# Top-k attention into a Fourier mixer: first scores from half of the queries and keys on two queues, and the tails' products padded to the full array

## The chip, the cores and the metric

The kernel runs on one core of a Trainium2 chip. The metric is device time in microseconds (us), as the median of several executions. The profile comes from one further execution. The engines of the core are TensorE (PE, with its weight loads listed as PEld), VectorE (DVE), ScalarE (ACT), GpSimd (POOL) and SyncE (SP), which issues most DMA transfers.

## The reference

All tensors are 32-bit floats. There are 8 batches, 8 heads, 576 tokens and a head size of 64. In the attention block each row of scores keeps its 32 largest entries:

```python
scores = scale * np.matmul(q, k.transpose(0, 1, 3, 2))          # 576 x 576 for each of 64 heads
kth = np.partition(scores, -32, axis=-1)[..., -32:-31]
scores = np.where(scores >= kth, scores, -1e9)
attn = np.exp(scores - scores.max(-1, keepdims=True))
attn = attn / (attn.sum(-1, keepdims=True) + 1e-9)
x = np.matmul(attn, v)                                           # -> (8, 576, 512)
```

The second block takes the real part of a two-dimensional Fourier transform over tokens and channels, adds it, normalises, and applies a two-layer MLP of 512 x 2048:

```python
u = x + np.real(np.fft.fft(np.fft.fft(x, axis=1), axis=2))
un = (u - u.mean(-1, keepdims=True)) / np.sqrt(u.var(-1, keepdims=True) + 1e-6)
out = u + np.maximum(un @ w_ch1, 0.0) @ w_ch2
```

## The kernel before, in words

**Tiles.** Two heads form a pair; there are 32 pairs, four to a batch. The 576 tokens of a head are two halves of 288, and each half is cut into two full blocks of 128 and a tail of 32. So a pair has full blocks 0 to 3 for each head, and block 4, which holds the tails. The tails' queries of both heads are handled as one item of 64 rows. A pair therefore has nine items (`IN_PAIR`), and the kernel walks over 288 items, one to a step of its main loop.

**One item.** `scores` (L274) multiplies queries by keys. Part 0 gives the scores against the four full key blocks (L329, and L314 for the tails' item from the second batch on). Part 1 (L299) gives the scores against the tails' keys of both heads at once: the right operand is `kt_t`, a block-diagonal 128 x 128 tile. For the tails' item its left operand has 64 columns, for others 128. ACT copies the scores from PSUM into the tile S (L332, L303). Then `top_ops` finds the 32 largest of each row on DVE, by four MAX8 (L350) and three MATCH_REPLACE8 (L352). `bounds` (L359, POOL) makes the thresholds `nt`; `mask` uses ACT (L366) and POOL (L367); `expo` is ACT's exponent (L373). `transposes` (L394, L405, L409) turns the result on PE, and `attend` (L431) multiplies by v.

**Order.** The schedule is written out by hand. In each step the program emits, engine by engine, the work of several items: the scores of item i+3, the first two top-k rounds of item i+1 and the last two of item i, the mask, the exponent, and work planned with `at(step, where, fn, cost)`. The loop fills PE up to a planned time per step (`level`) with pieces of the previous batch's MLP (`hidden`, L737, and `back`, L761 and L797). Each engine runs its own instructions in program order. In steps 0 to 33 the weights are also loaded and converted from 64-bit words: ACT writes `wh` (L169) and two more parts (L185, L188), DVE shifts (L176), POOL joins (L195, L196).

**Queries and keys.** `load_nat` brings the q or k of a pair into `nat_t`, one buffer that both share, with four transfers of 64 KB (`load_full`, L213) and four of 8 KB for the tails (`load_tails`, L224). `prep` (L239) transposes it on PE (L248) and copies it to `qT` (L256) or to `kT` (L258) and `kt_t` (L261) on ACT. Pair 0's k has a buffer of its own, `kn0`. At the start SP issues q of pair 0, the tails of pair 0's k, three weight pieces, v, then q of pair 1, and then the constants `fs`, `fd`, `sg` and two more weight pieces. ACT issues the identity and the full blocks of pair 0's k after its function table load (L844). In the loop, the q of the next pair is prepared in the first step of a pair.

**Token transform.** `dft_tokens` (L579) is called twice for a batch (even and odd frequencies). It multiplies folded tokens by the table `fs`: twelve products of 128 output rows and three with a single one. The third block of each sum is the tails', which has 64 rows; `fold_tails` (L535) writes it. ACT copies the result to `y` (L627 to L629), which `dft_channels` (L639) uses on PE (L651).

In the profile each of these matmuls appears as two passes, each with its own weight load.

Of the kernel before, what the change touches and what calls it, by code (L numbers as in the profile page):

```python
# [9 lines left out]
F32 = mybir.dt.float32  # L10
# [8 lines left out]
P = 128  # L19
TH = 32  # L20
# [44 lines left out]
def kernel(  # L65
# [9 lines left out]
    nc = tc.nc  # L75
    B, H, S, D = q.shape
# [4 lines left out]
    NC = 5  # L81
# [41 lines left out]
    nat_t = const.tile([P, NC, 2, D], F32, name="nat", tag="nat")  # L123

    kt_t = const.tile([P, P], F32, name="kt", tag="kt")
    v_t = [const.tile([P, NC, 2, D], F32, name=f"v{i}", tag=f"v{i}") for i in range(2)]


# [76 lines left out]

    def load_full(dst, src, pair, queue=None):
        b, hp = divmod(pair, NPB)
        for e in range(2):  # L210
            s2 = src[b, 2 * hp + e].rearrange("(h r) d -> h r d", h=2)
            for h in range(2):
                (queue or nc.sync).dma_start(  # L213
                    out=dst[:, 2 * h:2 * h + 2, e, :],
                    in_=s2[h, 0:2 * P, :].rearrange("(t p) d -> p t d", p=P),
                )

    def load_tails(dst, src, pair, row0=(0, 0)):
        b, hp = divmod(pair, NPB)
        for e in range(2):  # L220
            s2 = src[b, 2 * hp + e].rearrange("(h r) d -> h r d", h=2)
            for h in range(2):
                r0 = row0[e] + TH * h
                nc.sync.dma_start(out=dst[r0:r0 + TH, NF, e, :], in_=s2[h, 2 * P:HS, :])  # L224

    def load_nat(n, pair, dst=None, queue=None):
        if pair < NPAIR:
            nat[n, pair] = nat_t if dst is None else dst
            src = q if n == "q" else k
            load_full(nat[n, pair], src, pair, queue)  # L230
            load_tails(nat[n, pair], src, pair)

    def load_v(pair):
# [2 lines left out]
            load_full(v_of[pair], v, pair)  # L236
            load_tails(v_of[pair], v, pair, (0, TAIL))

    def prep(n, pair):  # L239

        if pair >= NPAIR:
            return 0.0
        src = nat.pop((n, pair))
        t_sb = attp.tile([P, S if n == "q" else NF * P], F32, name=f"{n}T_{pair}", tag=f"{n}T")
        for c0, c1 in ((0, NF), (NF, NC)):
            tp = ps_t.tile([P, 4, P], F32, name=f"tp{n}_{pair}_{c0}", tag="tp")
            for c in range(c0, c1):
                nc.tensor.transpose(  # L248
                    tp[:, c - c0, :], src[:, c, :, :].rearrange("p h d -> p (h d)"), ident
                )  # L250
            if c0 == 0:
                dst, got = t_sb[:, 0:NF * P], tp.rearrange("p a c -> p (a c)")
            else:
                dst, got = t_sb[:, NF * P:], tp[:, 0, 0:TAIL]
            if n == "q":
                nc.scalar.mul(out=dst, in_=got, mul=scale)  # L256
            elif c0 == 0:
                nc.scalar.copy(out=dst, in_=got)  # L258
            else:
                for hd in (slice(0, D), slice(D, P)):  # L260
                    nc.scalar.copy(out=kt_t[hd, hd], in_=got[hd])  # L261
        (qT_of if n == "q" else kT_of)[pair] = t_sb
        return 0.7


# [8 lines left out]
    def scores(i, part):  # L274

        if not 0 <= i < N:
            return 0.0
        pair, t, e = items[i]  # L280
        qT, kT = qT_of[pair], kT_of[pair]
        rows = ROWS[t]
        if part == 0:
            for n in range(1 if e is None else 2):
                Ssb[i + n] = attp.tile([P, S], F32, name=f"S_{i + n}", tag="S", bufs=6)
        q_cols = slice(P * t, P * t + rows)


        plain = (slice(0, NF * P), slice(NF * P, S))
        if e is None:  # L290
            to = [(Ssb[i], slice(TAIL * h, TAIL * (h + 1)), *plain) for h in range(2)]
        else:
            to = [
                (Ssb[i], slice(0, P), *plain),
                (Ssb[i + 1], slice(0, P), slice(TAIL, S), slice(0, TAIL)),
            ]
        if part == 1:
            sp = ps_s.tile([P, NF * P], F32, name=f"sp_{i}_t", tag="sp")
            nc.tensor.matmul(  # L299
                sp[0:rows, 0:P], lhsT=qT[:, q_cols], rhs=kt_t, start=True, stop=True  # L300
            )
            for h, (s_t, r, _, tails) in enumerate(to):
                nc.scalar.copy(out=s_t[r, tails], in_=sp[0:rows, TAIL * h:TAIL * (h + 1)])  # L303
            return 0.3
        if e is None and i >= PER_BATCH:

            half = NF * P // 2
            sps = [
                ps_s.tile([P, NF * P], F32, name=f"sp_{i}_{h}", tag="sp") for h in range(2)
            ]  # L310
            for g in range(2):
                for h in range(2):
                    hd = slice(D * h, D * (h + 1))
# [12 lines left out]
        for h, (s_t, r, keys, _) in enumerate(to):  # L326
            hd = slice(D * h, D * (h + 1))
            sp = ps_s.tile([P, NF * P], F32, name=f"sp_{i}_{h}", tag="sp")
            nc.tensor.matmul(  # L329
                sp[r], lhsT=qT[hd, q_cols], rhs=kT[hd, :], start=True, stop=True  # L330
            )
            nc.scalar.copy(out=s_t[r, keys], in_=sp[r])  # L332
        return 1.04
# [174 lines left out]
        return ap.rearrange("p (m two) -> p two m", two=2)  # L508

    Q1, Q2, Q3 = DM // 4, DM // 2, 3 * DM // 4  # L510
    ROWS3 = (P, P, TAIL)
    folded, ft_of, y_of, yt_of, us_of, rs_of, unT_of = ({} for _ in range(7))

    def fold_channels(eng, z, f, n):

# [18 lines left out]

    def fold_tails(b, eng):  # L535


        z = batp.tile([P, DM], F32, name=f"zt_{b}", tag="fold_s")[0:TAIL]
        ft_of[b] = batp.tile([P, DM + 1], F32, name=f"ft_{b}", tag="fold_t")
        f = ft_of[b][0:TAIL]  # L540
        fold_halves(eng, x_of[b][0:TAIL, 4, :], z)
        for n in range(2):
            fold_channels(eng, z, f[:, 0:DM], n)
        eng.tensor_copy(out=f[:, DM:DM + 1], in_=z[:, Q1:Q1 + 1])
# [34 lines left out]
    def dft_tokens(b, par):  # L579
# [1 line left out]
        while any(u[2] == "hidden" for u in queue):  # L581
            one_unit()
        _, zw, fg = folded[b, par]
        tails = ft_of[b]
        if b not in y_of:
            y_of[b] = batp.tile([P, 4, S], F32, name=f"y_{b}", tag="y")
        y = y_of[b]
# [4 lines left out]
        def mm(g2, gg, st, lhsT, rows, table, start=False):  # L592

            nc.tensor.matmul(  # L594
                yps[g2][0:rows, gg, :],
                lhsT=lhsT[0:ROWS3[st]],
                rhs=fs[0:ROWS3[st], table, par, st, :],
                start=start,
                stop=st == 2,
                skip_group_check=True,  # L600
            )

        for g2 in range(2):
            for gg in range(2):
                g = 2 * g2 + gg
                for st in range(2):
                    mm(
                        g2, gg, st, fg[:, st, P * g:P * (g + 1)], P, gg,  # L610
                        start=gg == 0 and st == 0,
                    )
        for st in range(2):
            mm(0, 1, st, zw[:, st, Q1:Q1 + 1], 1, 0)
        mm(0, 1, 2, tails[:, DM:DM + 1], 1, 0)
        for g2 in range(2):
            for gg in range(2):
                g = 2 * g2 + gg
                mm(g2, gg, 2, tails[:, P * g:P * (g + 1)], P, gg)

        mir, back = (
            (slice(HS + 2, S, 2), slice(KQ - 2, 0, -1)) if par == 0
# [218 lines left out]
    nc.vector.memset(cc[:, 0:1], -1.0)  # L841

    warm = small.tile([P, 1], F32, name="warm", tag="rd", bufs=6)
    nc.scalar.activation(out=warm, in_=cc[:, 0:1], func=AF.Exp)  # L844
    nc.vector.memset(cc[:, 1:2], FAR)
    for t in mv + den_t:
        nc.vector.memset(t, 1.0)

    kn0 = batp.tile([P, NC, 2, D], F32, name="kn0", tag="y")
    for t in v_t:  # L850
        nc.gpsimd.memset(t[TAIL:P, NF, 0, :], 0.0)
        nc.gpsimd.memset(t[0:TAIL, NF, 1, :], 0.0)
    for t in (nat_t, kn0):
        nc.gpsimd.memset(t[TAIL:P, NF, :, :], 0.0)
    nc.gpsimd.memset(kt_t, 0.0)

    nc.scalar.dma_start(out=ident, in_=id_d.ap())
    load_nat("q", 0)
    load_nat("k", 0, kn0, nc.scalar)
    prep("q", 0)  # L860
    prep("k", 0)


# [14 lines left out]
    for n in range(3):  # L878
        load(n)
    load_v(0)  # L880
    load_nat("q", 1)
    nc.sync.dma_start(out=fs, in_=fs_d.ap())
    nc.sync.dma_start(out=fd, in_=fd_d.ap())
    nc.sync.dma_start(out=sg, in_=sg_d.ap())
# [139 lines left out]
            got += one_unit()  # L1024
        return got

    for j in (0, 2):
        for c in range(2):
            scores(j, c)
    for op in top_ops(0, (0, 1)):  # L1030
        op()
    i, carry = 0, 0.0
# [144 lines left out]
```

## Time and profile before

| | |
|---|---|
| median of 8 executions | 1956.56 us (1955.75 to 1957.84) |
| profiled execution | 1956.7 us |
| its span, from first to last instruction | 1954.9 us |
| granted TensorE clock, mean | 0.972 |
| first MAX8 on DVE | 12.45 us after the span's start |
| first pass of the first token transform | 241.92 us |

The span is what the profiler's rows cover; the execution's own time is 1.8 us longer. A row of the timeline gives start, length, engine, line, operation, output and inputs; for PE the first shape, such as 128\*64, is the part of the array that is used (rows \* columns). What stands in brackets is the engine's idle time before the row and what ended it. `PEld` rows are weight loads, rows with a q after the engine (`SPq`) are its queue's instructions. Passes overlap in time, so the start of the next pass, not the end of the last one, tells what a pass costs.

### The profile page before, as it was taken

The numbers are of one execution on the slowest core, as the hardware profiler recorded it, in microseconds if no ns is written. First come the engines' busy times: TensorE is split into PE (matmuls) and PEld (weight loads), VectorE is DVE, ScalarE is ACT, GpSimd is POOL, SyncE is SP. The second block draws the span as 40 slices with busy tenths as digits, with TensorE's granted clock in tenths as the row PEclk, the third lists the DMA queues.
The fourth block names the chain that finished last, engine by engine and source line by source line (L and its number), as shares of the span: only waits on it lengthen the run. The fifth ranks groups of instructions, "written<-read, shape, count | busy, mean of one in ns | idle before, by whom it ended". The sixth has DMA issues, their size and how long they took to land.

```text
span 1954.9 us, 27234 instructions
## 1 busy us (share of the span) xinstructions
PE 1842.3 (94%) x8626; PEld 1116.0 (57%) x8626; DVE 1576.8 (81%) x3240; ACT 1202.6 (62%) x3063; POOL 773.3 (40%) x1056
## 2 busy tenths in 40 slices
PE   6566699999999999999999999999999999998999
PEld 3334465464655656556564756556564756566655
DVE  7999989998999989888888879988888879843000
ACT  6878657776766667666666657666666657541100
POOL 4768642326523444235523444235522444232000
PEclk8787799999999999999999999999999999999999
DMA  5333000101001010010100110010000100000000
GB/s 156 107 94 105 19 13 19 33 19 29 19 19 33 19 26 16 13 33 19 29 19 19 27 24 18 13 33 19 24 18 25 27 24 19 1 14 1 11 14 11
DMA packets 133583, 57.80 MB, mean 30 GB/s; under 512 B 124352, under 2 KB 124480, under 8 KB 133440
## 3 DMA queue, kind: packets, MB, share of 16 engines
q1 hardware_dynamic: 132208, 55.73, 10.6%
q8 instruction: 69, 1.13, 0.2%
q14 instruction: 74, 0.61, 0.1%
q10 hardware_dynamic: 1232, 0.33, 0.1%
HBM read 46.57 MB, written 9.44 MB: 29 GB/s over the span
## 4 chain that ended last, share of the span: by engine, by line
PE 80%; POOL 7%; DVE 6%; issue 3%; ACT 3%; DMA 0%; SPq 0%; POOLq 0%; DVEq 0%; ACTq 0%
PE hp L737 24%; PE cp L761 22%; PE o L431 7%; PE tpP L394 6%; PE sp L329 6%; PE yp L594 3%; PE cp L797 3%; POOL wk L367 2%; PE mp L651 2%; DVE m L350 2%; DVE wk L352 2%; PE sp_t L299 2%; POOL w L196 2%; POOL w L195 2%; PE tpk L248 1%
## 5 line engine op out<-in xcount | busy, mean ns | idle before, releaser
L367 POOL TENSOR_TENSOR wk<-S,wk 128x576 f32<-128x576 f32 x288 | 407.0, 1413 | 919.2 <-ACT wk L366 865.6
L350 DVE MAX8 m<-wk 128x8 f32<-128x576 f32 x864 | 623.4, 749 | 5.5
L737 PE MATMUL hp<-unT,w 128*128 128x256 f32 (+1 forms) x2048 | 539.5, 410 | 2.5 <-ACT unT L718 2.1
L761 PE MATMUL cp<-w,hT 128*128 128x512 f32 x1024 | 478.4, 599 | 0.0
L737 PEld LDWEIGHTS hp<-unT,w 128*128 128x128 f32 x2048 | 373.4, 191 | 126.6 <-issue 32.3
L352 DVE MATCH_REPLACE8 wk<-m,wk 128x576 f32<-128x576 f32 x576 | 427.6, 742 | 0.0
L761 PEld LDWEIGHTS cp<-w,hT 128*128 128x128 f32 x1024 | 179.3, 190 | 182.3 <-issue 181.5
L373 ACT ACTIVATE wk<-wk,nt 128x576 f32<-128x576 f32 x288 | 224.8, 781 | 53.6 <-POOL wk L367 52.2
L394 PE MATMUL tpP<-ident,wk 128*128 128x128 f32 x1152 | 185.3, 285 | 67.3 <-ACT wk L373 45.1
L397 ACT COPY PT<-tpP 128x512 f32<-128x512 f32 (+1 forms) x320 | 171.0, 545 | 123.8 <-PE tpP L394 121.3
L366 ACT ACTIVATE wk<-S,nt 128x576 f32<-128x576 f32 x288 | 226.9, 788 | 27.0 <-POOL nt L359 25.8
L394 PEld LDWEIGHTS tpP<-ident,wk 128*128 128x128 f32 x1152 | 139.7, 145 | 166.9 <-ACT wk L373 63.4
L350 DVE MAX8 m<-S 128x8 f32<-128x576 f32 x288 | 214.0, 743 | 22.6 <-ACT S L303 22.3
L741 ACT ACTIVATE hT<-hp 128x320 f32<-128x320 f32 (+1 forms) x256 | 104.7, 409 | 197.4 <-PE hp L737 195.1
L352 DVE MATCH_REPLACE8 wk<-m,S 128x576 f32<-128x576 f32 x288 | 213.7, 742 | 0.0
L431 PE MATMUL o<-PT,v 128*64 128x256 f32 (+3 forms) x1440 | 193.4, 411 | 2.2 <-ACT PT L397 1.7
L332 ACT COPY S<-sp 128x512 f32<-128x512 f32 (+1 forms) x264 | 141.9, 588 | 65.9 <-PE sp L329 65.7
L329 PE MATMUL sp<-kT,qT 64*128 64x512 f32 (+1 forms) x528 | 161.0, 671 | 3.6 <-ACT means L916 3.1
L431 PEld LDWEIGHTS o<-PT,v 128*64 128x64 f32 x1440 | 110.1, 151 | 75.0 <-issue 16.1
L775 DVE SCALAR_TENSOR_TENSOR x<-cp,gi,x 128x512 f32<-128x512 f32 x11 | 8.2, 746 | 128.3 <-PE cp L761 128.3
L299 PEld LDWEIGHTS sp_t<-kt,qT 128*128 128x128 f32 (+1 forms) x322 | 51.3, 186 | 58.4 <-issue 22.2
L329 PEld LDWEIGHTS sp<-kT,qT 64*128 64x128 f32 (+1 forms) x528 | 42.7, 192 | 60.8 <-issue 44.7
(124 smaller groups left out, 1797.5 us busy)
## 6 DMA issues: line engine op xcount, KB each, us to landing
space<-in_moe_w_ch_dram SPq DMA_DIRECT2D x32, 512.0 KB, 3.6
nat<-in_q_dram SPq DMA_DIRECT2D x128, 64.0 KB, 2.1
v<-in_v_dram SPq DMA_DIRECT2D x128, 64.0 KB, 2.1
out_dram<-x SPq DMA_DIRECT2D x32, 256.0 KB, 2.1
nat<-in_k_dram SPq DMA_DIRECT2D x124, 64.0 KB, 2.1
nat<-in_q_dram SPq DMA_DIRECT2D x128, 8.0 KB, 1.7
v<-in_v_dram SPq DMA_DIRECT2D x128, 8.0 KB, 1.7
nat<-in_k_dram SPq DMA_DIRECT2D x124, 8.0 KB, 1.7
```

What stands on the lines that cost most here:

```text
L329: nc.tensor.matmul(sp[r], lhsT=qT[hd, q_cols], rhs=kT[hd, :], start=True, stop=True)
L332: nc.scalar.copy(out=s_t[r, keys], in_=sp[r])
L350: ops.append(lambda src=src, m8=m8: nc.vector.max(out=m8, in_=src))
L352: ops.append(lambda src=src, m8=m8: nc.vector.match_replace(w, m8, src, NEG))
L366: nc.scalar.activation(out=w, in_=Ssb[i], func=AF.Relu, scale=-FAR, bias=Nt[i][:, 1:2])
L367: nc.gpsimd.tensor_tensor(out=w, in0=Ssb.pop(i), in1=w, op=ALU.subtract)
L373: nc.scalar.activation(out=w, in_=w, func=AF.Exp, bias=Nt.pop(i)[:, 0:1], accum_out=den_t[pair % 3][:, c:c + 1],)
L394: nc.tensor.transpose(tp[:, c, :], p_sb[:, k0 + P * c:k0 + P * (c + 1)], ident)
L397: nc.scalar.copy(out=pt[:, NF * he:NF * (he + 1), col:col + w], in_=tp[:, :, o:o + w])
L431: nc.tensor.matmul(o[D * e:D * (e + 1), c0:c1], lhsT=vv[:, c, e, :], rhs=pt[:, 2 * NF if c == NF else NF * e + c, c0:c1], start=(c == 0), ...
L737: nc.tensor.matmul(hp[:, 0:w], lhsT=w1[:, dt, P * it:P * (it + 1)], rhs=unT[:, dt, 0:w], start=(dt == 0), stop=(dt == NDT - 1),)
L761: nc.tensor.matmul(cp, lhsT=hT[:, it, P * n:P * (n + 1)], rhs=w2[:, it, :], start=(it == 0), stop=(it == NIT - 1),)
```

## The change

The start is put in another order. Of pair 0, SP now issues the first halves of q, the first halves of k, one head's k tails, the second halves of q and the q tails; ACT issues the identity, the second halves of k and the other head's k tails, and all this before ACT's function table is loaded. `prep` is split, so that only query blocks 0 and 1 are transposed ahead of the first scores; blocks 2, 3 and the tails follow after the scores of items 0 and 1. The q loads of pair 1 are emitted after that, and so stand on SP behind `fs`, `fd`, `sg` and the two weight pieces. Item 0's product with the tails' keys uses another PSUM pool and is copied by DVE. The memsets of `nat_t`, `kn0` and `kt_t` go from POOL to DVE.

The tails' item takes the last 128 columns of `qT` as its left operand, so that its 64 rows come out as rows 64 to 127. The tails of the token transform get a constant tile of 128 rows, `ftail`, which POOL zeroes once and of which `fold_tails` writes the first 64 rows, and all products use 128 rows; each tails' product follows its group's other two, and the three one-column products come last.

```diff
+    ftail = const.tile([P, DM + 1], F32, name="ftail", tag="ftail")
...
+    def load_half(dst, src, pair, e, h, queue=None):
...
-    def prep(n, pair):
+    def prep(n, pair, blocks=((0, NF), (NF, NC))):
...
-        for c0, c1 in ((0, NF), (NF, NC)):
+        for c0, c1 in blocks:
...
-            sp = ps_s.tile([P, NF * P], F32, name=f"sp_{i}_t", tag="sp")
+            pool, tag = (ps_s, "sp") if i else (ps_m, "mm")
+            copy = nc.scalar.copy if i else nc.vector.tensor_copy
+            sp = pool.tile([P, NF * P], F32, name=f"sp_{i}_t", tag=tag)
+            q_end = P * t + rows
             nc.tensor.matmul(
-                sp[0:rows, 0:P], lhsT=qT[:, q_cols], rhs=kt_t, start=True, stop=True
+                sp[:, 0:P], lhsT=qT[:, q_end - P:q_end], rhs=kt_t, start=True, stop=True
             )
             for h, (s_t, r, _, tails) in enumerate(to):
-                nc.scalar.copy(out=s_t[r, tails], in_=sp[0:rows, TAIL * h:TAIL * (h + 1)])
+                copy(out=s_t[r, tails], in_=sp[P - rows:P, TAIL * h:TAIL * (h + 1)])
...
-        ft_of[b] = batp.tile([P, DM + 1], F32, name=f"ft_{b}", tag="fold_t")
-        f = ft_of[b][0:TAIL]
+        f = ftail[0:TAIL]
...
-                lhsT=lhsT[0:ROWS3[st]],
-                rhs=fs[0:ROWS3[st], table, par, st, :],
+                lhsT=lhsT,
+                rhs=fs[:, table, par, st, :],
...
-                for st in range(2):
-                    mm(
-                        g2, gg, st, fg[:, st, P * g:P * (g + 1)], P, gg,
-                        start=gg == 0 and st == 0,
-                    )
-        for st in range(2):
-            mm(0, 1, st, zw[:, st, Q1:Q1 + 1], 1, 0)
-        mm(0, 1, 2, tails[:, DM:DM + 1], 1, 0)
-        for g2 in range(2):
-            for gg in range(2):
-                g = 2 * g2 + gg
-                mm(g2, gg, 2, tails[:, P * g:P * (g + 1)], P, gg)
+                for st in range(3):
+                    f = fg[:, st] if st < 2 else ftail
+                    mm(g2, gg, st, f[:, P * g:P * (g + 1)], P, gg, start=gg == 0 and st == 0)
+        for st in range(3):
+            mm(0, 1, st, zw[:, st, Q1:Q1 + 1] if st < 2 else ftail[:, DM:DM + 1], 1, 0)
...
     warm = small.tile([P, 1], F32, name="warm", tag="rd", bufs=6)
+    kn0 = batp.tile([P, NC, 2, D], F32, name="kn0", tag="y")
+    for t in (kn0, nat_t):
+        nc.vector.memset(t[TAIL:P, NF, :, :], 0.0)
+    nc.vector.memset(kt_t, 0.0)
+
+    nat["q", 0], nat["k", 0] = nat_t, kn0
+    nc.scalar.dma_start(out=ident, in_=id_d.ap())
+    for e in range(2):
+        load_half(nat_t, q, 0, e, 0)
+    for e in range(2):
+        load_half(kn0, k, 0, e, 1, nc.scalar)
+        load_half(kn0, k, 0, e, 0)
+    load_tails(kn0, k, 0, queue=nc.scalar, heads=(0,))
+    load_tails(kn0, k, 0, heads=(1,))
+    for e in range(2):
+        load_half(nat_t, q, 0, e, 1)
+    load_tails(nat_t, q, 0)
     nc.scalar.activation(out=warm, in_=cc[:, 0:1], func=AF.Exp)
...
-    for t in (nat_t, kn0):
-        nc.gpsimd.memset(t[TAIL:P, NF, :, :], 0.0)
-    nc.gpsimd.memset(kt_t, 0.0)
-
-    nc.scalar.dma_start(out=ident, in_=id_d.ap())
-    load_nat("q", 0)
-    load_nat("k", 0, kn0, nc.scalar)
-    prep("q", 0)
+    nc.gpsimd.memset(ftail, 0.0)
+    prep("q", 0, ((0, 2),))
     prep("k", 0)
...
     load_v(0)
-    load_nat("q", 1)
     nc.sync.dma_start(out=fs, in_=fs_d.ap())
...
-    for j in (0, 2):
-        for c in range(2):
-            scores(j, c)
+    for c in range(2):
+        scores(0, c)
+    prep("q", 0, ((2, NF), (NF, NC)))
+    load_nat("q", 1)
+    for c in range(2):
+        scores(2, c)
     for op in top_ops(0, (0, 1)):
         op()
```

More of the change, by code (lines that the diff above doesn't have):

```diff
@@ L202, with load_full, load_tails @@
     x_of, o_of, xT_of, rd_of = ({} for _ in range(4))
-    def load_full(dst, src, pair, queue=None):
+    def load_half(dst, src, pair, e, h, queue=None):
         b, hp = divmod(pair, NPB)
+        s2 = src[b, 2 * hp + e].rearrange("(h r) d -> h r d", h=2)
+        (queue or nc.sync).dma_start(
+            out=dst[:, 2 * h:2 * h + 2, e, :],
+            in_=s2[h, 0:2 * P, :].rearrange("(t p) d -> p t d", p=P),
+        )
+    def load_full(dst, src, pair):
         for e in range(2):
-            s2 = src[b, 2 * hp + e].rearrange("(h r) d -> h r d", h=2)
             for h in range(2):
-                (queue or nc.sync).dma_start(
-                    out=dst[:, 2 * h:2 * h + 2, e, :],
-                    in_=s2[h, 0:2 * P, :].rearrange("(t p) d -> p t d", p=P),
-                )
-    def load_tails(dst, src, pair, row0=(0, 0)):
+                load_half(dst, src, pair, e, h)
+    def load_tails(dst, src, pair, row0=(0, 0), queue=None, heads=(0, 1)):
         b, hp = divmod(pair, NPB)
-        for e in range(2):
+        for e in heads:
             s2 = src[b, 2 * hp + e].rearrange("(h r) d -> h r d", h=2)
@@ L223, in load_tails, with load_nat @@
                 r0 = row0[e] + TH * h
-                nc.sync.dma_start(out=dst[r0:r0 + TH, NF, e, :], in_=s2[h, 2 * P:HS, :])
-    def load_nat(n, pair, dst=None, queue=None):
+                (queue or nc.sync).dma_start(
+                    out=dst[r0:r0 + TH, NF, e, :], in_=s2[h, 2 * P:HS, :]
+                )
+    def load_nat(n, pair):
         if pair < NPAIR:
-            nat[n, pair] = nat_t if dst is None else dst
+            nat[n, pair] = nat_t
             src = q if n == "q" else k
-            load_full(nat[n, pair], src, pair, queue)
+            load_full(nat[n, pair], src, pair)
             load_tails(nat[n, pair], src, pair)
@@ L237, in load_v @@
             load_tails(v_of[pair], v, pair, (0, TAIL))
-    def prep(n, pair):
+    def prep(n, pair, blocks=((0, NF), (NF, NC))):
         if pair >= NPAIR:
             return 0.0
-        src = nat.pop((n, pair))
-        t_sb = attp.tile([P, S if n == "q" else NF * P], F32, name=f"{n}T_{pair}", tag=f"{n}T")
-        for c0, c1 in ((0, NF), (NF, NC)):
+        src, got_of = nat[n, pair], qT_of if n == "q" else kT_of
+        if pair not in got_of:
+            got_of[pair] = attp.tile(
+                [P, S if n == "q" else NF * P], F32, name=f"{n}T_{pair}", tag=f"{n}T"
+            )
+        t_sb = got_of[pair]
+        for c0, c1 in blocks:
             tp = ps_t.tile([P, 4, P], F32, name=f"tp{n}_{pair}_{c0}", tag="tp")
@@ L250, in prep @@
                 )
-            if c0 == 0:
-                dst, got = t_sb[:, 0:NF * P], tp.rearrange("p a c -> p (a c)")
+            if c0 < NF:
+                dst, got = t_sb[:, c0 * P:c1 * P], tp.rearrange("p a c -> p (a c)")[:, 0:(c1 - c0) * P]
             else:
@@ L256, in prep @@
                 nc.scalar.mul(out=dst, in_=got, mul=scale)
-            elif c0 == 0:
+            elif c0 < NF:
                 nc.scalar.copy(out=dst, in_=got)
             else:
-                for hd in (slice(0, D), slice(D, P)):
-                    nc.scalar.copy(out=kt_t[hd, hd], in_=got[hd])
-        (qT_of if n == "q" else kT_of)[pair] = t_sb
+                for e in range(2):
+                    r = slice(D * e, D * (e + 1))
+                    nc.scalar.copy(out=kt_t[r, TAIL * e:TAIL * (e + 1)], in_=tp[r, 0, 0:TAIL])
         return 0.7
@@ L510 @@
     Q1, Q2, Q3 = DM // 4, DM // 2, 3 * DM // 4
-    ROWS3 = (P, P, TAIL)
-    folded, ft_of, y_of, yt_of, us_of, rs_of, unT_of = ({} for _ in range(7))
+    folded, y_of, yt_of, us_of, rs_of, unT_of = ({} for _ in range(6))
     def fold_channels(eng, z, f, n):
@@ L583, in dft_tokens @@
         _, zw, fg = folded[b, par]
-        tails = ft_of[b]
         if b not in y_of:
@@ L607, in dft_tokens @@
                 g = 2 * g2 + gg
-                for st in range(2):
-                    mm(
-                        g2, gg, st, fg[:, st, P * g:P * (g + 1)], P, gg,
-                        start=gg == 0 and st == 0,
-                    )
-        for st in range(2):
-            mm(0, 1, st, zw[:, st, Q1:Q1 + 1], 1, 0)
-        mm(0, 1, 2, tails[:, DM:DM + 1], 1, 0)
-        for g2 in range(2):
-            for gg in range(2):
-                g = 2 * g2 + gg
-                mm(g2, gg, 2, tails[:, P * g:P * (g + 1)], P, gg)
+                for st in range(3):
[3 more added lines that the diff above has]
+            mm(0, 1, st, zw[:, st, Q1:Q1 + 1] if st < 2 else ftail[:, DM:DM + 1], 1, 0)
         mir, back = (
@@ L843 @@
     warm = small.tile([P, 1], F32, name="warm", tag="rd", bufs=6)
+    kn0 = batp.tile([P, NC, 2, D], F32, name="kn0", tag="y")
[11 more added lines that the diff above has]
+    load_tails(kn0, k, 0, heads=(1,))
+    for e in range(2):
+        load_half(nat_t, q, 0, e, 1)
+    load_tails(nat_t, q, 0)
     nc.scalar.activation(out=warm, in_=cc[:, 0:1], func=AF.Exp)
@@ L847 @@
         nc.vector.memset(t, 1.0)
-    kn0 = batp.tile([P, NC, 2, D], F32, name="kn0", tag="y")
     for t in v_t:
```

## The prediction

> **What bounds the kernel now.** I began with the page: its busy shares and its chain of waits.
>
> ```profile
> PE 1842.3 (94%) x8626; PEld 1116.0 (57%) x8626; DVE 1576.8 (81%) x3240; ACT 1202.6 (62%) x3063; POOL 773.3 (40%) x1056
> PE 80%; POOL 7%; DVE 6%; issue 3%; ACT 3%; DMA 0%; SPq 0%; POOLq 0%; DVEq 0%; ACTq 0%
> ```
>
> TensorE (PE) looks like the limit, but the average hides two regimes. The table of stages separates them (columns: stage, its length, busy time of PE, PE's weight loads, DVE, ACT, POOL, then the granted clock).
>
> ```profile
> 12.00:140.00 128.00, 84.08 (x393) 50.53 (x392) 126.17 (x257) 101.66 (x237) 78.92 (x79) 0.78 0.38 116
> 140.00:237.00 97.00, 62.92 (x323) 38.13 (x323) 91.43 (x185) 73.98 (x178) 72.94 (x78) 0.79 0.23 68
> 260.00:600.00 340.00, 329.49 (x1601) 198.51 (x1600) 319.86 (x660) 241.09 (x640) 142.10 (x201) 0.99 0.10 23
> 600.00:1200.00 600.00, 595.30 (x2888) 359.94 (x2887) 532.00 (x1099) 399.39 (x1027) 251.05 (x361) 1.00 0.09 23
> ```
>
> In batch 0 (to 237 us) PE works 65% of the time and DVE 94 to 99%; from 260 us on PE is full (595.30 of 600) and DVE has slack. So a PE saving counts after 237 us, and a start-up change counts only through whatever paces batch 0. I read the timeline for both.
>
> **Part 1: the tails' score product, padded from 64 to 128 columns.** PE's timeline around one of them (start, length, instruction, tile shape of the array, passes; each program matmul is two passes):
>
> ```profile
> 700.70 0.59 PE L761 MATMUL cp<-w,hT 128*128 128x512 f32 x1
> 701.22 0.43 PE L299 MATMUL sp_t<-kt,qT 128*64 128x128 f32 x2
> 701.58 0.70 PE L761 MATMUL cp<-w,hT 128*128 128x512 f32 x1
> ```
>
> In an unbroken stream the passes of cp follow one another after 0.43 us (the loader's rows at 447.99 and 448.42). Here the pass before sp_t holds PE 0.52: 0.09 for entering shape 128*64. The two sp_t passes take 0.36 until cp returns at 701.58; the same product in shape 128*128 takes 0.23 (693.97 to 694.20, below), so 0.13 to 0.14. The returning pass lasts 0.70 instead of 0.59, 0.11 more. Together 0.34 us. Where transposes follow (0.109 us a pass), less of the last term shows and I read 0.29. All of it goes when sp_t keeps the shape of its neighbours. There are 32 such products; four stand in batch 0 and one at its end, where PE has slack. Of the other 27, 18 are followed by MLP products and 9 by transposes: 18 x 0.34 + 9 x 0.29 = 8.7 us.
>
> [...] The rows count the wide load too (the 0.23 above includes it, hidden behind the pass before), so the sum uses the rows.
>
> **Part 2: the token transform, 16 calls.** The tails move to 128 rows and stand behind their group's other two products; the three one-column products come last.
>
> ```profile
> 689.09 2.25 PE L594 MATMUL yp<-fs,fg 128*128 128x145 f32 x16
> 691.27 0.66 PE L594 MATMUL yp<-fs,zw 128*1 128x145 f32 x4
> 691.86 1.58 PE L594 MATMUL yp<-fs,ft 64*1 64x145 f32 x10
> 693.37 0.66 PE L394 MATMUL tpP<-ident,wk 128*128 128x128 f32 x4
> 693.97 0.39 PE L299 MATMUL sp_t<-kt,qT 128*128 128x128 f32 x2
> 694.20 0.59 PE L761 MATMUL cp<-w,hT 128*128 128x512 f32 x1
> ```
>
> A call lasts 4.28 us (689.09 to 693.37) in four shapes. A pass takes 0.122 us. The change of shape at 691.86 costs 0.09 (four zw passes need 0.59 instead of 0.49). That from 64*1 to 64*128, seen as 0.25 us of an idle loader in its rows at 692.19, costs 0.09 and another 0.105 for the uncovered first load. Both vanish; the change to 128*1 and the way back to 128*128 stay. 0.29 x 16 = 4.6 us. One thing is given back: the first output bank now gets its last product at the call's end, not about 0.46 us before it, so its ACT copies start later. That matters where the next PE work waits for them: after batch 0's two calls and at 1797.41 in the last batch, where PE's row shows 0.47 us idle on ACT's copy of y. I subtract 0.9.
>
> PE is thus shorter by 8.7 + 4.6 - 0.9 = 12.4 us. Not all of it reaches the end: between 260 and 1720 us the chain has DVE's two top-k lines at 4.7% and some POOL and issue time. PE's 80% of 1954.9 is 1564 us, at most 0.91 of the 1718 us after 237. I take 0.9: **11.2 us**. Upper end 12.4 (PE idle is about 18 us of 1460); lower end half, 6.2, since DVE is at 94% from 260 to 600.
>
> **Part 3: the start.** The first scores now need half of q, all of k and the identity. DVE's first MAX8 starts at 12.45; the scores' product starts at 8.57, when kT is copied. In the new order six 64 KB loads stand ahead instead of eight and both queues share k, so k is issued by about 2.6 and lands by 5.0 (such loads land a median 2.4 us after issue in the first 50 us), instead of the 6.62 at which its transposes begin now; ACT loads its table after five issues (about 3.2 to 4.5), still before the first copy. Each following step keeps its row, and the tails' scores no longer wait for a free bank (0.76 at 11.41), with DVE copying them. First MAX8 at about 10: 2.5 us earlier; bounds 0 (table load late) and 3.5. The memsets moved to DVE and POOL lie before 12.45, in DVE's 11.25 idle us and POOL's 17.3; were either busy they would cost under 0.6.
>
> But pair 1's query loads are moved, too. On SP they used to stand ahead of fs, fd, sg and two weight loads; now they stand behind them. SP's rows:
>
> ```profile
> 14.66 1.92 SPq L213 DMA_DIRECT2D nat<-in_q_dram  x4
> 18.52 0.42 SPq L882 DMA_DIRECT2D fs<-c_fs  x1
> 21.40 2.20 SPq L213 DMA_DIRECT2D nat<-in_k_dram  x4
> 24.72 3.11 SPq L224 DMA_DIRECT2D nat<-in_k_dram  x4
> ```
>
> Before, the k loads of pair 1 stood exactly where the q loads stand now. Their median landing is 6.0 us after issue (tails 3.3), because they follow 2.4 MB on the same queue: the last full one lands about 28.4, the last tail about 29.1, that is 9.9 and 10.6 us after fs was issued. fs will be issued at about 14.8 in q's old place, so q of pair 1 lands at about 24.7 and 25.4. Who waits:
>
> ```profile
> 19.17 0.60 ACT L256 ACTIVATE qT<-tpq 128x512 f32<-128x512 f32 x1 [2.62 <-PE tpq L248]
> 20.27 0.22 ACT L256 ACTIVATE qT<-tpq 128x64 f32<-128x64 f32 x1 [0.50 <-PE tpq L248]
> 20.39 0.77 ACT L366 ACTIVATE wk<-S,nt 128x576 f32<-128x576 f32 x1
> 21.05 0.62 ACT L169 ACTIVATE wh<-space 128x512 f32<-128x512 f32 x1
> ```
>
> ACT copies pair 1's q before it masks tile 0, in the new program's order as well. Behind those copies on ACT queue the mask, the weight conversion and the exponent. Transposes from 24.7 take 1.19, the copies end at 26.5, the mask starts there instead of 20.39: **6.1 us later**, though its bounds are ready sooner. POOL's subtraction and weight joins follow the mask, and the next bounds follow the joins: mask, 1.42, 1.29, 1.29, 0.2 is a ring of 5.07 us a tile (masks at 31.42, 36.48, 41.56) that runs beside DVE's 5.55 and keeps its delay. DVE takes the converted weight at 25.80 with 4.1 us to spare (wh ends 21.67), so DVE first loses its lead and stops about 2.4 us late. The ring recovers only where it waits for DVE: 0.6 and 0.45 us at 86.98 and 92.53. From 139 us the ring itself is the limit (at 151.65 DVE waits 0.52 for wh), as POOL has the centring as well. So 6.1 - 1.1 = **5.0 us** of delay reach the end of batch 0. Bounds: 6.1 if nothing is absorbed, and minus 2.5 if the ring does not carry it and DVE's early start counts.
>
> **Sum.** -11.2 + 5.0 = -6.2 us. The profiled execution is 1956.7 (span 1954.9 and 1.8 around it), 0.1 above the median of 1956.56; the forecast is 1950.4.
>
> **Rivals.**
> - *The start gain survives* (pair 1's q lands early enough, or ACT's delay is absorbed): -11.2 - 2.5, 1942.9. For it: DVE is 99% busy to 140 us and has no gap then. Against: ACT works in program order and k's rows show where a load at that place lands.
> - *Half the PE saving is lost to DVE*, with the same delay: -6.2 + 5.0, 1955.4. For it: 94% DVE from 260 to 600 and top-k lines in the chain. Against: 88% after 600.
> - *Slower*: DVE, not PE, paces the batches, so that a shorter PE only waits longer for the masked tiles, and the late q is all that remains: 1961.6. It decides once less than 5.0 of 12.4 us, 40%, comes through. For it: PE already waits for ACT's exponent in places (5.0 us in seven waits from 260 to 1720). Against: PE's gaps there are about 1%.
> - *The change does not do what it says* at the start: the first MAX8 stays near 12.4 because ACT's table load delays the first copy. It changes little, since the ring decides: within 0.5 us of the forecast.
>
> **Chances.** A measurement here can tell about 0.2%, 3.9 us, from no change. Forecast (with the last rival) 0.55, of it 0.08 within 3.9 us; start gain survives 0.20; half lost 0.13, of it 0.10 within; slower 0.12. Faster 0.70, same 0.18, slower 0.12. The range takes the first rival's time and reaches past the half-lost case: 1942.5 to 1957.
>
> **What would show it.** Right: no shape 128*64 or 64*128 in the rows of sp_t and yp; a transform call of 4.0 us; passes around the tails' product back at 0.43 and 0.23; first MAX8 near 10; the transposes of pair 1's q near 25, ACT's first mask near 26.5; the first transform call (241.92 before) 5 us later. Wrong: that call at 240 or earlier, which is the first rival; or PE's idle time from 260 to 1720 grown by over 6 us, which is the second or third.

## The result

| | median | runs | profiled execution | its span |
|---|---|---|---|---|
| before | 1956.63 us (1955.75 to 1959.16) | 28 | 1956.7 us | 1954.9 us |
| after | 1951.07 us (1949.05 to 1952.1) | 10 | 1949.95 us | 1948.2 us |

The ratio is 0.997, with a 95% interval of 0.9962 to 0.9978: 5.6 us faster, where the forecast was 6.2. From here on, line numbers are those of the kernel that is named.

The page of the kernel after, busy times and the chain of waits by engine:

```profile
PE 1827.4 (94%) x8626; PEld 1120.7 (58%) x8626; DVE 1578.1 (81%) x3245; ACT 1201.6 (62%) x3062; POOL 772.7 (40%) x1054
PE 79%; POOL 8%; DVE 5%; issue 4%; ACT 3%; DMA 1%; SPq 0%; POOLq 0%; ACTq 0%; DVEq 0%
```

PE has as many instructions and is busy 14.9 us less. The weight loads take 4.7 us more in all, and they lie beside PE's passes. The table of stages (length, busy PE, PE's loads, DVE, ACT, POOL, then clock, DMA share and GB/s) shows the same two regimes as before: batch 0 paced by DVE and its partners, PE full after it.

```profile
12.00:140.00 128.00, 77.44 (x364) 46.95 (x364) 121.31 (x248) 96.98 (x227) 76.33 (x76) 0.71 0.37 114
140.00:237.00 97.00, 65.03 (x333) 40.73 (x332) 91.41 (x184) 74.53 (x177) 74.80 (x80) 0.75 0.25 73
260.00:600.00 340.00, 328.46 (x1607) 201.78 (x1606) 321.05 (x662) 239.78 (x638) 140.90 (x200) 0.99 0.09 22
600.00:1200.00 600.00, 594.66 (x2922) 364.20 (x2923) 536.50 (x1109) 402.22 (x1033) 253.82 (x365) 1.00 0.09 23
```

In the first stage DVE is 4.9 us less busy (126.17 to 121.31). The timeline of the start tells why:

```profile
10.05 0.76 DVE L367 MAX8 m<-S 128x8 f32<-128x576 f32 x1
...
14.83 0.42 SPq L895 DMA_DIRECT2D fs<-c_fs  x1
...
17.69 2.29 SPq L214 DMA_DIRECT2D nat<-in_q_dram  x4
...
20.96 3.32 SPq L230 DMA_DIRECT2D nat<-in_q_dram  x4
...
24.79 1.31 PE L260 MATMUL tpq<-ident,nat 128*128 128x128 f32 x5 [11.82 <-DMA nat<-in_q_dram]
...
25.91 0.71 ACT L268 ACTIVATE qT<-tpq 128x512 f32<-128x512 f32 x2 [12.53 <-PE tpq L260]
...
26.51 0.78 ACT L383 ACTIVATE wk<-S,nt 128x576 f32<-128x576 f32 x1
27.17 0.63 ACT L171 ACTIVATE wh<-space 128x512 f32<-128x512 f32 x1
...
27.83 0.69 DVE L178 TENSOR_SCALAR w<-wh 128x512 int32<-128x512 int32 x1 [4.34 <-ACT wh L171]
```

The same DVE instruction in the kernel before, without a gap ahead of it:

```profile
25.80 0.68 DVE L176 TENSOR_SCALAR w<-wh 128x512 int32<-128x512 int32 x1
```

The first MAX8 is 2.4 us earlier. But pair 1's queries are issued at 17.69 instead of 14.66, and PE waits 11.82 us for them. ACT then has nothing to copy for 12.53 us, and the mask of tile 0, behind the copies in ACT's program order, starts at 26.51 instead of 20.39. The bracket at 27.83 is the bill: DVE stands 4.34 us for the weight that ACT converts after that mask. The first transform call starts at 246.50 (before: 241.93): 4.6 us late.

PE's rows around one padded tails' product, and those of a token transform:

```profile
702.32 0.59 PE L766 MATMUL cp<-w,hT 128*128 128x512 f32 x1
702.75 0.38 PE L316 MATMUL sp_t<-kt,qT 128*128 128x128 f32 x2
702.97 0.59 PE L766 MATMUL cp<-w,hT 128*128 128x512 f32 x1
```

```profile
246.50 0.76 PE L607 MATMUL yp<-fs,fg 128*128 128x145 f32 x4
...
249.33 0.41 PE L607 MATMUL yp<-fs,ftail 128*128 128x145 f32 x2
249.67 0.66 PE L607 MATMUL yp<-fs,zw 128*1 128x145 f32 x4
250.17 0.41 PE L607 MATMUL yp<-fs,ftail 128*1 128x145 f32 x2
250.51 0.76 PE L607 MATMUL yp<-fs,fsp 128*128 128x145 f32 x4
...
255.08 0.70 PE L656 MATMUL mp<-fd,y 128*128 128x256 f32 x2 [0.50 <-ACT y L632]
```

The pass ahead of `sp_t` gives PE up after 0.43 us (0.52 before), the two passes take 0.22 (0.36), and the returning pass lasts 0.59 (0.70): 0.34 us a product. The loader's rows, before and after, show where the weight load of `sp_t` lies. Before, it begins together with the product's first pass (701.22); now it begins at 702.48, beside the pass of cp, 0.27 us ahead of the product:

```profile
701.22 0.19 PEld L299 LDWEIGHTS sp_t<-kt,qT 128*64 128x64 f32 x2 [0.76 <-ACT S L321]
```

```profile
702.48 0.46 PEld L316 LDWEIGHTS sp_t<-kt,qT 128*128 128x128 f32 x2 [0.40 <-ACT S L338]
```

A call takes 4.01 us (246.50 to 250.51, where the next one begins). The bracket at 255.08 shows what is given back: after batch 0's two calls `mp` waits 0.50 us for the copy of y (0.01 before). In the last batch, at 1790.63, the same wait is 0.96 (0.47 before, at 1797.41):

```profile
1797.41 1.99 PE L651 MATMUL mp<-fd,y 128*128 128x256 f32 x8 [0.47 <-ACT y L629]
```

```profile
1790.63 1.99 PE L656 MATMUL mp<-fd,y 128*128 128x256 f32 x8 [0.96 <-ACT y L634]
```

### The profile page after: what moved, and what is told of

Its sections match the earlier page's. It is cut to its first block, busy times and chain, and to the rows that moved or that the text cites. A ratio compares the mean times of both kernels' runs of the same rounds, so it can differ in the third digit from the quotient of the medians.

```text
span 1948.2 us, 27231 instructions
## 1 busy us (share of the span) xinstructions
PE 1827.4 (94%) x8626; PEld 1120.7 (58%) x8626; DVE 1578.1 (81%) x3245; ACT 1201.6 (62%) x3062; POOL 772.7 (40%) x1054
## 4 chain that ended last, share of the span: by engine, by line
PE 79%; POOL 8%; DVE 5%; issue 4%; ACT 3%; DMA 1%; SPq 0%; POOLq 0%; ACTq 0%; DVEq 0%
PE hp L742 24%; PE cp L766 22%; PE o L448 7%; PE sp L346 6%; PE tpP L411 5%; PE yp L607 3%; PE cp L802 3%; POOL wk L384 3%; PE mp L656 2%; DVE m L367 2%; POOL w L198 2%; POOL w L197 2%; PE sp_t L316 2%; DVE wk L369 2%; PE tpq L260 1%
## 5 line engine op out<-in xcount | busy, mean ns | idle before, releaser
L367 DVE MAX8 m<-S 128x8 f32<-128x576 f32 x288 | 214.1, 743 | 12.4 <-ACT S L320 12.1
L316 PEld LDWEIGHTS sp_t<-kt,qT 128*128 128x128 f32 x322 | 56.4, 196 | 50.5 <-issue 20.2
```

What stands on the lines that cost most here:

```text
L367: ops.append(lambda src=src, m8=m8: nc.vector.max(out=m8, in_=src))
```

## Experiments

The theory: the paddings shorten PE by 12.4 us and most of that comes through after 242 us; the late queries of pair 1 cost about 5 us, because ACT's program order carries their delay into a ring of mask, subtraction, joins and bounds. The rivals: the start is worth something by itself; DVE takes half of the PE saving; part of the loss has another cause than the queries. In all, twelve kernels ran, in three groups; the kernel before stood at 1956.84, 1957.03 and 1956.74 us in them.

**The two halves of the change, alone.** `pad_only` is the kernel before with both paddings, `start_only` the changed kernel with both taken back (the main lines):

```diff
 # pad_only, against before
-                sp[0:rows, 0:P], lhsT=qT[:, q_cols], rhs=kt_t, start=True, stop=True
+                sp[:, 0:P], lhsT=qT[:, q_end - P:q_end], rhs=kt_t, start=True, stop=True
...
-                mm(g2, gg, 2, tails[:, P * g:P * (g + 1)], P, gg)
+                for st in range(3):
+                    f = fg[:, st] if st < 2 else ftail
+                    mm(g2, gg, st, f[:, P * g:P * (g + 1)], P, gg, start=gg == 0 and st == 0)
 # start_only, against after: the same lines the other way round
```

> The start is as before; only the tails' score product and the token transform are padded. Theory (PE paces the batches, the start costs 4.6 us): the transform's first call starts where it did before (241.9 us), all later gain stays, about 11.3 us, so 1945.3. Rival (DVE paces the batches, the padding is worth little and the new start brings the gain): within 3 us of before, 1954 or more.

> Only the new start; both paddings are taken back. Theory (late q of pair 1 delays ACT's first mask to 26.5 us, the ring of mask, subtraction, joins and bounds carries it): first MAX8 near 10, first call of the transform 4.6 us later than before, time 1961.2. Rival (the earlier first MAX8 counts): 2.5 us faster than before, 1954.1.

`pad_only` took 1945.31 us (ratio 0.994, 0.9927 to 0.9953), `start_only` 1960.96 (1.0021, 1.0012 to 1.003). So the paddings bring 11.5 us and the new start, though its first MAX8 is at 10.10, costs 4.1; its first mask stands at 25.69 and its first transform at 246.73. Together they would make 7.4 us; the change brings 5.6. The intervals of the three ratios are wider than that gap, so it stays open whether the two really disturb each other. In the profiled executions a part of it can be placed: `start_only`'s masks are 4.80 us behind those of before at 262 us and 3.24 behind at 276, where the trace of before has a stretch with PE at half its clock (granted clock 0.50 from 263.58 to 266.99) and that of `start_only` has none. Such stretches are looked at below.

**Where pair 1's queries are loaded.** Three kernels are the changed one with this place moved: `q_early` as before the change, `q_mid` between old and new, and `q_own` into a buffer of their own, so that they need not wait until pair 0's are transposed. In the first two, the scores of item 0 and the rest of `prep` for pair 0's q are emitted earlier as well, since these loads overwrite the buffer.

```diff
 # q_early: the scores of item 0 and prep("q", 0, ...) moved up behind prep("k", 0), and then
     load_v(0)
+    load_nat("q", 1)
     nc.sync.dma_start(out=fs, in_=fs_d.ap())
 # q_mid: the same, but
     nc.sync.dma_start(out=sg, in_=sg_d.ap())
+    load_nat("q", 1)
 # q_own
     load_tails(nat_t, q, 0)
+    qn1 = batp.tile([P, NC, 2, D], F32, name="qn1", tag="fold_s")
+    nc.vector.memset(qn1[TAIL:P, NF, :, :], 0.0)
+    nat["q", 1] = qn1
+    load_full(qn1, q, 1)
+    load_tails(qn1, q, 1)
...
-    load_nat("q", 1)
```

> The change with pair 1's q loads back in their old place on SP, ahead of fs, fd, sg and two weight loads; the first scores and the second half of pair 0's q are emitted ahead of them. Theory: q of pair 1 lands by 20 us, the first mask starts at 20.3 as before, the delay of batch 0 falls from 4.6 us to between 0 and -1, time 1945 to 1946.5. Rival (the delay came from the start's other edits, such as the table load behind the DMA issues): as the change, 1951.

> The change with a buffer of its own for pair 1's q, loaded on SP right behind pair 0's q tails, ahead of the weights and v. Theory: the first mask no longer waits for q and starts when its bounds are ready, near 17.3 us, 3 us earlier than before; the ring's lead is cut to DVE's lead of 2.4 us, so the first call of the transform starts near 239.5 and the time is 1943. Rival (the weight loads, now some 4 us later, or a ring that waits elsewhere take the lead back): no better than 1945.

> As the run with pair 1's q in its old place, but behind fs, fd and sg and ahead of the two weight loads: a middle dose of the delay. Theory: q lands by 23, the first mask starts at 23.6 to 24, so the first call of the transform lies between 243 and 244.5 and the time is 1948.3. Rival (the delay has a threshold, so that a mask 3.4 us late costs nothing): 1945, as with q in its old place.

| kernel | first mask | first transform | median | ratio |
|---|---|---|---|---|
| q_own | 17.13 | 238.78 | 1943.49 | 0.9931 (0.9918 to 0.9944) |
| q_early | 19.69 | 240.29 | 1944.98 | 0.9938 (0.9924 to 0.9952) |
| q_mid | 24.08 | 244.46 | 1948.32 | 0.9955 (0.9943 to 0.9968) |
| after | 26.51 | 246.50 | 1951.07 | 0.997 (0.9962 to 0.9978) |

The times came within 0.5 us of the forecasts; `q_early`'s first transform is 1.6 us ahead of that of before, where up to 1 was expected. Four places of one load, and the time follows the first mask at 0.8 us for each us (7.6 of 9.4). The first transform follows it at the same rate. That the cause is this load, and not the split `prep` or another part of the new start, is thereby shown: `q_own` differs from the changed kernel in nothing but the load, its buffer and that buffer's memset (the loads that stand behind it on SP move with it). The timeline of `q_own`'s start:

```profile
7.35 1.96 SPq L214 DMA_DIRECT2D qn<-in_q_dram  x4
...
9.99 0.76 DVE L367 MAX8 m<-S 128x8 f32<-128x576 f32 x1
...
17.13 0.78 ACT L383 ACTIVATE wk<-S,nt 128x576 f32<-128x576 f32 x1 [2.50 <-POOL nt L376]
...
23.34 0.68 DVE L178 TENSOR_SCALAR w<-wh 128x512 int32<-128x512 int32 x1
```

The mask now waits for its bounds (POOL), not for the copies of q, and DVE's first shift has no bracket: DVE runs through, 2.46 us ahead of before up to 131 us and 3.1 ahead from 150 to 250. This is the version that the change was one buffer away from. In its group it stands 13.35 us under the kernel before. It also stands 1.8 us under `pad_only`, which has the old start, but the two intervals overlap: that the new start is worth something of its own, even with early queries, is not shown.

**The paddings one by one.** `sp_only` has the padded score product alone, `dft_only` the padded transform alone (the two halves of the diff of `pad_only`).

> Before, with only the tails' score product padded to 128 columns. Theory (27 products outside batch 0, 0.34 or 0.29 us each, 0.9 of it reaching the end): 7.8 us faster, 1949.0. [...]

> Before, with only the token transform padded and reordered. Theory: a call of 4.00 instead of 4.28 us, 16 times 0.28, less 1.0 us for PE's waits on the copies of y: 3.3 us faster, 1953.5. Rival (the waits on the copies eat it up): within 1 us of before.

`dft_only` took 1953.78 us (0.9983, 0.9974 to 0.9992), as expected. `sp_only` took 1951.26 (0.9971, 0.9959 to 0.9982): 5.8 us instead of 7.8, though a product in its trace is 0.34 us shorter. The time stands 2.3 us above the theory (1949.0). Its interval reaches 8.0 us, so the shortfall is not clear of noise by itself. Nor, by the intervals, is the gap between the 9.0 us that the paddings bring one by one and the 11.5 of `pad_only`. The trace shows a place for the loss, though. Against the trace of before, its MAX8s are 1.28 us ahead at 457 us and 0.54 behind at 545; from 280 us to that stretch and after it they gain steadily. In the stretch, PE's timeline and a table of windows (columns as above; the clock is the number before the last two) show:

```profile
481.61 0.65 PE L395 MATMUL tpP<-ident,wk 128*128 128x128 f32 x4 [2.22 <-ACT wk L374]
...
496.11 1.28 PE L248 MATMUL tpq<-ident,nat 128*128 128x128 f32 x5 [1.23 <-ACT PT L398]
```

```profile
475.00:482.50 7.50, 5.28 (x26) 2.88 (x28) 6.75 (x14) 6.56 (x21) 3.25 (x2) 1.00 0.01 3
482.50:485.90 3.40, 3.40 (x16) 1.64 (x14) 3.37 (x8) 0.16 (x1) 3.13 (x4) 0.51 0.16 63
485.90:496.20 10.30, 7.96 (x48) 4.91 (x47) 8.53 (x18) 7.25 (x21) 6.14 (x11) 1.00 0.01 5
496.20:499.60 3.40, 3.40 (x13) 2.98 (x14) 1.53 (x4) 2.28 (x8) 1.55 (x2) 0.50 0.19 43
```

After an idle gap of 2.22 us PE ran at half its clock for 3.4 us (0.51 in the table), and again at 496.2 (0.50), after a gap of 1.23. The trace of before has the same gaps (2.20 at 480.5, 1.23 at 496.0) and no such stretch there. That the clock alone makes the loss is not shown: `pad_only` and `dft_only` have the stretch near 482 too, and their MAX8s gain 0.8 and 0.9 us on before between 470 and 508 us.

**The order inside the transform.** `old_order` is the change with the tails' products behind the one-column products again, on 128 rows:

```diff
-                for st in range(3):
-                    f = fg[:, st] if st < 2 else ftail
-                    mm(g2, gg, st, f[:, P * g:P * (g + 1)], P, gg, start=gg == 0 and st == 0)
+                for st in range(2):
+                    mm(g2, gg, st, fg[:, st, P * g:P * (g + 1)], P, gg, start=gg == 0 and st == 0)
...
+        for g2 in range(2):
+            for gg in range(2):
+                g = 2 * g2 + gg
+                mm(g2, gg, 2, ftail[:, P * g:P * (g + 1)], P, gg)
```

> The change with the old order inside the token transform (one-column products in the middle, tails' products last), all on 128 rows. The shapes change as often as in the change. Theory: calls stay at 4.00 us, PE's two waits on the copies of y (0.50 and 0.96 us in the change) return to 0.01 and 0.47, time 0.9 us under the change, 1950.2. Rival (the order, not the shape, saves the time): calls of 4.2 us, 1953 or more.

It took 1950.36 us (0.9967, 0.9955 to 0.998), 0.7 under the change, less than can be told apart. The waits on y, in batch 0 and in the last one, are back at 0.02 and 0.47 us, as expected. The calls did not stay at 4.00 us, though: they take 4.10 where they took 4.00, since the way back from one column to 128 now lies inside the call (PE's loader stands idle 0.25 us there, at 248.3). In the changed order the way back comes after the call, and I read it as a cost of the product that follows; no run takes it alone.

**PE's idle gaps, filled.** To price the half-speed stretches, four kernels got throw-away products in the gaps at 262 and 480 us: `before_fill`, `sp_fill`, `pad_fill` and `own_fill`, made from before, `sp_only`, `pad_only` and `q_own`.

```diff
             tp = ps_t.tile([P, 4, P], F32, name=f"tpP_{i}", tag="tp")
+            for _ in range(2 if i == 77 else 0):
+                nc.tensor.matmul(tp.rearrange("p c k -> p (c k)"), lhsT=ident, rhs=w1[:, 0, 0:NF * P], start=True, stop=True)
...
             hp = ps_m.tile([P, CW[0]], F32, name=f"hp_{b}_{ch}_{it}", tag="mm")
+            for _ in range(3 if idle else 0):
+                nc.tensor.matmul(hp, lhsT=ident, rhs=w1[:, 0, 0:CW[0]], start=True, stop=True)
```

> The kernel before, with throw-away products (identity times a piece of w1) put on PE in two of its idle gaps: two of 512 columns ahead of the transposes of item 77 (gap 2.20 us at 480.5), three of 320 ahead of the first MLP product of batch 0 (gap 2.08 at 261.7); their results are overwritten. Theory A: PE's granted clock halves for 3.41 us after a stretch of 3.41 us with PE under half busy (seen after the first gap in 9 of the ten traces so far, after the second in 7), and each such half-speed stretch takes up to 1.7 us from the PE-bound part; without them the time falls by about 2.4 us, to 1954.4, and the clock shows no drop near 264 and 482. Theory B: DVE is 94% busy there and hides it, so the time stays at 1956.8 or rises by what the added products push back (under 0.5 us).

> The kernel before with the score product of the tails padded (sp_only, 1951.3) and the same throw-away products. If two half-speed stretches (at 482.5 and 496.2 in the profiled execution of sp_only) are why the padding alone brought 5.8 and not 7.8 us, this stands 7.8 us under before_fill. If the missing 2 us have another cause, it stands 5.8 under it.

> The kernel before with both paddings (pad_only, 1945.3) and the same throw-away products. Theory A: about 2.4 us under pad_only, 1942.9. Theory B: 1945.3. Its distance to before_fill should be the 11.5 us of pad_only against before if the clock does not enter the price of the paddings, and 12.4, the whole PE saving, if it does.

> The change with pair 1's queries in a buffer of their own and loaded early (q_own, 1943.5), and the same throw-away products. Theory A: 1941.1, and no half-speed stretch near 260 and 479. Theory B: 1943.5.

| | without | with the products | ratio to before |
|---|---|---|---|
| before | 1956.74 | 1957.19 | 1.0003 (0.9994 to 1.0013) |
| sp_only | 1951.26 | 1949.85 | 0.9965 (0.9952 to 0.9978) |
| pad_only | 1945.31 | 1944.89 | 0.994 (0.9927 to 0.9953) |
| q_own | 1943.49 | 1942.69 | 0.9929 (0.9916 to 0.9942) |

Theory A's size is refuted. The stretch near 264 us is gone from all four traces, and the one near 482 as well; yet the times fall by 0.5 us on average, not by 2.4, and that of before rose by 0.45; none of the four differences is clear of noise. Two reasons can be read. First, a stretch is cheaper than thought: in `before_fill` the lead over before grows by 0.70 us where the one at 264 is gone and shrinks by 0.69 where it has one that before has not (at 488.6), and `sp_only` lost 1.8 over its two, so 0.7 to 0.9 each in these two traces and not 1.7 (the masks of `start_only` gained 1.6 on before where before alone has one). Second, a third gap was left open, ahead of batch 1's transform (PE's timeline of `before_fill`, and the same passes in before):

```profile
489.21 3.61 PE L599 MATMUL yp<-fs,fg 128*128 128x145 f32 x16 [2.75 <-POOL fg L522]
```

```profile
490.04 2.94 PE L594 MATMUL yp<-fs,fg 128*128 128x145 f32 x16 [2.75 <-POOL fg L517]
```

The clock fell at 488.6 in this trace, and the 16 passes last 3.61 us instead of 2.94; `sp_fill` lost it at the same place (mean clock 0.83 from 485.9 to 496.2). `pad_fill` and `own_fill` have the same gap and no half-speed stretch at all between 240 and 1700 us, and still their medians are only 0.4 and 0.8 us better, so the second reason does not reach these two.

Between kernels with the products, the paddings come nearer to the working: `sp_fill` is 7.3 us under `before_fill` (7.8 expected) and `pad_fill` 12.3 under it (12.4). The intervals do not tell 7.3 from 5.8. So the half-speed stretches are a likely reason for `sp_only`'s missing 2 us, not a shown one. Against it stands that all six of its runs lie within 0.65 us, though such a stretch stands in one trace and not in another; that they all met both is not shown.

`own_fill` is the fastest kernel of the study, but it can't be told from `q_own`.

## Why the prediction was right

**Part 1, the score product.** 0.34 us between MLP products was predicted and 0.34 measured. In `sp_only` 5.8 of the 7.8 us came; the likely reason is given above. PE's loads of `sp_t` grew by 5.1 us in all (56.4 us, 51.3 before), but the two wide passes take 0.22 us against 0.36 for the narrow ones, and the wide load lies beside the pass before it (702.48).

**Part 2, the transform.** 4.0 us a call predicted, 4.01 measured. The 0.9 us given back was 0.98: 0.49 more at each of the two waits that the prediction named, after batch 0's calls and in the last batch.

**The transfer to the end.** 11.2 us after the first transform was predicted; between that call and the end of the span the change gains 11.3 (a lag of 4.6 us becomes a lead of 6.7). `pad_only` gives 11.5 by itself. The rival that DVE takes half of it, and the slower one that DVE paces the batches, fall with this: PE's idle time from 260 to 1720 us grew only from 17.6 to 19.6.

**Part 3, the start.** First MAX8 about 10, measured 10.05; the queries' transposes at 24.7, measured 24.79; first mask at 26.5, measured 26.51; DVE's first stop about 2.4 us late, measured 2.0 (27.83 against 25.80). The rows that stood for this were those of the k loads, which had been in the same place of the queue. The ring carried the delay as read: 6.12 us at the first mask, still 6.08 at tile 11, and then 4.95 at tile 13, behind the two places named (86.98 and 92.53). Tile 15 falls to 3.79, which was not foreseen, the lag then moves between 3.5 and 4.9, and from tile 35 to the transform it is 4.6. So 1.55 us were absorbed and not 1.1, and 4.6 us reached the transform, not 5.0.

**What was off.** The median is 0.7 us above the forecast, although the profiled execution (1949.95) is 0.45 below it and its trace has every term of the sum within 0.5. The prediction went from a profiled execution that was 0.1 from its median; for the changed kernel it is 1.1 us below. The rival called "the start gain survives" named 1942.9 for queries that land early enough: `q_own` makes them land so, and took 1943.49. That the sum came within 0.7 us is in part luck: measured one by one, the halves make 7.4 us and not 5.6, and the paddings alone 9.0 and not 11.5, so the terms are known less well than the total was hit.

## What to carry to other kernels

A load that is moved has to be priced by the queue that it lands behind and by the instructions that stand behind its consumer on that engine: here the queries of one pair, issued 3 us later behind five other loads, took back more than half of what the two parts can bring (5.6 us instead of 13.35), and a buffer of their own gave it back. A PE saving counts where PE is full (`pad_only` brought 11.5 of 12.4 us), and a start-up saving can be lost at a later wait (`start_only` has its first MAX8 2.35 us earlier and takes 4.1 us longer); read both from a table of stages, not from the shares of the page. The small product in a shape of its own cost its neighbours as well as itself (0.09 us in the pass before and 0.11 in the one after, of 0.34), so price such a product from the start of the pass before it to the end of the pass after.

## What the runs showed that was not expected

PE's granted clock fell to 0.50 after idle gaps of only 1.23 to 2.75 us (`sp_only` at 496.2, `before_fill` at 488.6). In the ten traces of the first two groups and the two kernels compared, every half-speed stretch that ends before the trace does is a multiple of 3.41 us long, and each begins on a grid of 3.41 us, whose phase differs from one execution to the next (0.42 to 3.30 us after the span's start; 0.75 in the trace of before, 3.23 in that of the kernel after). I cut each trace along that grid into cells, starting at its first record of the granted clock, and counted:

| cell | PE busy in it | next cell at half speed, ten traces | before and after alone |
|---|---|---|---|
| full clock | under 40% | 133 of 133 | 23 of 23 |
| full clock | 40 to 65% | 36 of 82 | 8 of 22 |
| full clock | above 65% | 3 of 5078 | 0 of 1014 |
| half speed | under 85% | 159 of 161 | 36 of 36 |
| half speed | above 85% | 8 of 178 | 3 of 34 |

These are counts from the profiler's records of the granted clock and of PE; what sets the clock is not shown by them. They go with batch 0, where PE is 60 to 67% busy, having a mean clock of 0.71 to 0.79.

They also fit that much the same gap is followed by a stretch in one trace and not in another. The stretch near 264 us is in nine of the ten traces, that near 482 in six (not seven, as was put down ahead of `before_fill`). The four kernels with throw-away products all have the gap of 2.75 us ahead of batch 1's transform: where the grid leaves a cell 37% or 19% busy (`before_fill`, `sp_fill`) the clock fell, where the emptiest cell is 53% busy (`pad_fill`, `own_fill`) it didn't. Between 40 and 65% the busy share alone did not decide (36 of 82).
